# Selective attention and a GELU layer: v before w_in, absmax inside the first layer, batch 1's preparation moved forward

## The chip, the cores and the metric

The kernel runs on one core of one Trainium2 chip. The core has TensorE (PE: matmuls, and weight loads that overlap them), VectorE (DVE), ScalarE (ACT), GpSimd (POOL) and SyncE (SP), each with its own in-order queue of instructions; 16 DMA engines move data, and here GpSimd and SyncE issue nearly all transfers. The metric is the device time of one execution in microseconds; the median of several runs counts. The profile comes from one further execution, taken by the hardware profiler.

## The reference

There are 8 batches of 8 heads, 576 tokens and a head size of 64. The attention's bias falls with the sum of a gate s between two tokens. Its output, 4608 rows of 512, goes through two matrices with a GELU between them.

```python
scores = scale * q @ k.T                       # per head, scale = 1/8
cum = cumsum(maximum(s, 0))                    # along the tokens
scores = where(causal, -1e9, scores + minimum(-(cum[i] - cum[j]), 0))
attn = softmax(scores) @ v                     # exp, sum + 1e-9, divide
x = attn as [B*S, H*D]                         # [4608, 512]
g = 0.5*h*(1 + erf(h/sqrt(2))),  h = x @ w_in  # w_in [512, 2048]
out = g @ w_out                                # w_out [2048, 512]
```

All inputs are fp32, and so is the output.

## The kernel before

The bias splits into a factor of the row, which the softmax's division takes out, and a factor exp(cum[j]) of the column. The kernel makes that factor once for all heads (`cum_sum`, `weights`: a scan on VectorE, transposes on PE with the identity `ident`, exps on ScalarE into `wb`), multiplies v with it (`scale_v`, one VectorE instruction for each of five 128-token tiles, the last of 64 tokens), and keeps the factor itself as a 65th column (`den_col`), so that one matmul gives numerator and denominator. A check of the inputs' sizes guards the split. It needs the largest absolute value of q and k (`absmax`, two VectorE instructions a batch) and the sum of v squared (`square_v`, five ScalarE instructions a batch); a general path, not taken here, stands behind it.

A batch's attention is cut into four score units (g, u): g is one of two groups of four heads, u the first two or the last three token tiles. A unit is: `sc` (matmuls into two PSUM tiles of the tag "sc", of which there are two, and two exps on ScalarE into P), `mk` (the causal mask on VectorE), and `av` items, one for each g and token tile `it` (matmuls of P with the scaled v into a PSUM tile of the tag "av", also two, then a reciprocal and a multiplication on VectorE into x). When both groups of a tile are done, `to_xT` turns x, by PE and a copy or by a DMA transpose on SyncE's queue. q and k are turned by VectorE (`tr_qk`, four transposes a batch) from `raw_qk`, of which there are two buffers; `raw_v` also has two. A buffer's next load waits for all that read it.

The dense part goes in nine chunks of 512 tokens. In chunk c the first layer has eight items `l1_item` (two of 16 column blocks each, 8 matmuls and a GELU on ScalarE); in chunk 0 each item is cut into halves of 256 tokens, because x arrives in pieces. The second layer runs sixteen matmuls for each of four row blocks; `groups` cuts it into pieces and puts the side work of the next batch, b = c + 1, between them from lists `side[i]`. In chunk 0 row blocks 0 and 1 go together in eight groups of four matmuls; group i needs the w_out piece i // 2. Batch 0's attention is written out ahead of chunk 0, with `filler` matmuls on zeros (128x512) in PE's waits.

The order on each engine is that of the text (a manual schedule). GpSimd issues the loads of q, k, v, w_in and w_out; each cast to bf16 but v. It waits for the eighth load before, because eight semaphores go round. Until batch 0's k is cast, the first half of batch 0's k (`k_st`, loaded by SyncE as fp32) lies in batch 0's raw_v buffer, so the v loads over it wait for `cast_k0`. Two GpSimd selects make `ident` and the mask's triangle `uptri`. ScalarE loads an activation table at each change between exp and GELU (`exp_set`, `gelu_set`).

Of the kernel before, what the change touches and what calls it, by code (L numbers as in the profile page):

```python
# [19 lines left out]
def kernel(  # L20
# [10 lines left out]
    nc = tc.nc  # L31
# [10 lines left out]
    ST = 5  # L42
# [62 lines left out]
    def load_qk(b, i, g):  # L105
        t = raw_qk(b)
        for h in range(4):
            nc.gpsimd.dma_start(
                out=t[h * 32 : h * 32 + 32, i, g, :].rearrange("p (t c) -> p t c", c=2 * D),
                in_=qk_runs(q if i == 0 else k, b * H + 2 * h + g, 1),  # L110
            )
# [10 lines left out]
    def raw_v(b):  # L122
        raws[b, "v"] = work.tile([128, ST, H, D], fp32, tag="rawv", bufs=2, name="raw_v")
        return raws[b, "v"]
# [12 lines left out]
            )  # L137


    k_st = raw_v(0).rearrange("p s h d -> p (s h d)")[:, : S * 2]  # L140

    def load_k0():
        for h in range(4):
# [25 lines left out]

    zero = const.tile([128, NB], bf16, name="zero")  # L170
    nc.vector.memset(zero, 0.0)  # L171
    ident = const.tile([128, 128], fp32, name="ident")
    nc.vector.memset(ident, 0.0)
    make_identity(nc, ident, nomemset=True)
# [3 lines left out]
        out=uptri, in_=uptri, compare_op=ALU.is_gt, fill=1.0, base=0, pattern=[[-1, 128]],  # L178
        channel_multiplier=1,
    )  # L180
    load_qk(0, 1, 1)
    amx = const.tile([128, B * HG, 2], fp32, name="amx")
    wb = const.tile([128, ST, BH], bf16, name="wb")
    xT = const.tile([128, NP, n_tok], bf16, name="xT")
# [18 lines left out]
    def masks():  # L203
        nc.vector.tensor_copy(ident_bf, ident)
        nc.vector.tensor_copy(tri_bf, uptri)
# [33 lines left out]
    def den_col(b):  # L239
        nc.vector.tensor_copy(vv[b % 2][:, :, :, D], wb[:, :, b * H : (b + 1) * H])  # L240
# [181 lines left out]
    def filler(n, lhsT=None):  # L422

        f_ps = yps.tile([128, NB], fp32, tag="mlp", bufs=2, name="f_ps")
        for _ in range(n):
            nc.tensor.matmul(  # L426
                f_ps, lhsT=zero[:, :128] if lhsT is None else lhsT, rhs=zero, start=True, stop=True
            )

    def av_item(b, g, it, later=False):  # L430
        P = P_of[b, g]
        n = 128 if it < ST - 1 else SL
        o_ps = ps.tile([128, 4, D + 1], fp32, tag="av", bufs=2, name="av")
        for h in range(4):
            for i, (jt, off) in enumerate(BLK[it]):
                nc.tensor.matmul(  # L436
                    o_ps[:, h, :],
                    lhsT=P[:, h, off : off + 128],
                    rhs=vv[b % 2][:, jt, 2 * h + g, :],
                    start=(i == 0), stop=(i == len(BLK[it]) - 1),  # L440
                )
        if g == 0:
            x_of[b, it] = work.tile([128, H * D], bf16, tag="x", bufs=6, name="x")
        rc = work.tile([128, 4], fp32, tag="rc", bufs=3, name="rc")
        nc.vector.reciprocal(rc[:n], o_ps[:n, :, D])  # L445
        nc.vector.tensor_tensor(  # L446
            x_of[b, it][:n, :].rearrange("p (h g d) -> p g h d", g=HG, d=D)[:, g],
            o_ps[:n, :, 0:D],
            rc[:n].unsqueeze(2).to_broadcast([n, 4, D]),
            op=MULT,  # L450
        )
        if g == HG - 1 and b > 0 and not later:
            to_xT(b, it)
# [57 lines left out]


    exp_set()
    filler(18)
    cum_sum()
    weights()
    den_col(0)
    filler(10)
    cast_k0()

    filler(5, raws[0, "qk"][:, 1, 0, :128])
    load_v(0, nc.gpsimd, (0, 1))
    load_w(0, 0)
    load_w(0, 1)
    load_v(0, nc.gpsimd, (2, 3))
    load_w(0, 2)
    load_w(0, 3)
    load_v(0, nc.gpsimd, (4,))
    load_qks(1)
    load_w(1, 0)  # L530
    load_w(1, 1)
# [6 lines left out]
    tr_qk(0, 0, 1)  # L538
    tr_qk(0, 1, 1)
    masks()  # L540
    filler(2)
    sc_first(1, 0, (0,))
    scale_v(0, 0)
# [6 lines left out]
    sc_first(0, 1, (0,))  # L550
    av_item(0, 0, 1)
    filler(1)
    av_item(0, 1, 0)
    sc_first(0, 1, (1,))
    av_item(0, 1, 1)
    filler(1)
    to_xT(0, 0, True)
    sc_first(1, 1, (0,))
    to_xT(0, 1, True)
    filler(1)  # L560
    sc_first(1, 1, (1,))
    mk_item(0, 0, 1)
    scale_v(0, 2)
# [10 lines left out]
    for c in range(NCH):  # L574
        b = c + 1
        if c > 0 and b + 1 < B:
            load_qks(b + 1)
            load_v(b + 1, nc.gpsimd)
        if c == 0:

            late = [
                [], [(av, 0, 0, 2)], [], [(av, 0, 1, 2)], [(av, 0, 0, 3)],
                [(av, 0, 1, 3), (to_xT, 0, 2, True)], [(to_xT, 0, 3, True)],
                [], [(scale_v, 0, 4)], [], [(av, 0, 0, 4)], [(av, 0, 1, 4), (to_xT, 0, 4)],
            ] + [[]] * 4
            for half in range(2):
                for f2 in range(FT // 2):
                    l1_item(0, f2, half * 256, half * 256 + 256)
                    for f, *a in late[8 * half + f2]:
                        f(*a)  # L590
                    if f2 % 2 and 3 <= 8 * half + f2 <= 9:
                        square_v(0, 4 * half + f2 // 2 - 1)
            for g in range(HG):
                absmax(0, g)
        else:
            for f2 in range(FT // 2):
                l1_item(c, f2)
                for g, it in late_of.get(c, [])[f2 : f2 + 1]:
                    av(c, g, it)
                if b < B and f2 < HG:  # L600
                    tr_qk(b, 0, f2)
                    tr_qk(b, 1, f2)
                if b < B and f2 == 2:
                    den_col(b)
                    for st in range(2):
                        scale_v(b, st)
                if b < B and f2 == 3:
                    for st in range(2, ST):
                        scale_v(b, st)
                if b < B and 4 <= f2 < 4 + HG:  # L610
                    absmax(b, f2 - 4)
                if c == 2 and f2 == 7:
                    cert_decay()
                if c == 1 and 1 <= f2 <= ST:
                    square_v(c, f2 - 1)
        if b < B:
            if c == 0:
                for g in range(HG):
                    for i in range(2):
                        tr_qk(b, i, g)  # L620
                den_col(b)
            exp_set()
            if c == 0:
                side = [[] for _ in range(16)]
                side[0] = [(sc, b, 0, 0), (mk, b, 0, 0)]
                side[2] = [(sc, b, 1, 0), (mk, b, 1, 0)]
                side[3] = [
                    (sc, b, 0, 1), (scale_v, b, 0),
                    (av, b, 0, 0), (scale_v, b, 1), (av, b, 0, 1), (sc, b, 1, 1), (av, b, 1, 0),
                    (scale_v, b, 2), (av, b, 1, 1), (mk, b, 0, 1), (scale_v, b, 3),  # L630
                ]
                side[5] = [(av, b, 0, 2), (mk, b, 1, 1)]
                side[6] = [(av, b, 0, 3)]
                side[8] = [(av, b, 1, 2), (gelu_set,), (square_v, 0, 4)]
                side[9] = [(av, b, 1, 3), (scale_v, b, 4)]
                groups(c, (0, 1), side[:8])
                for sub in (2, 3):
                    groups(c, (sub,), side[4 * sub : 4 * sub + 4])
                load_qks(2)
                load_v(2, nc.gpsimd)  # L640
                for g in range(HG):
                    absmax(b, g)
            else:

                side = [[] for _ in range(16)]
                sc_at = (2, 5, 7, 9) if b < 4 else (2, 5, 8, 11)
                for at, (g, u) in zip(sc_at, [(0, 0), (1, 0), (0, 1), (1, 1)]):
                    side[at].append((sc, b, g, u))
                for st in range(ST):
                    side[sc_at[3]].append((square_v, b, st))  # L650
                side[sc_at[3]].append((gelu_set,))
                for at, (g, u) in zip((5, 8, 10 if b < 4 else 11, 12 if b < 4 else 14), [(0, 0), (1, 0), (0, 1), (1, 1)]):
                    side[at].append((mk, b, g, u))
                for at, (g, it) in zip((6, 7, 9, 10), [(0, 0), (0, 1), (1, 0), (1, 1)]):
                    side[at].append((av, b, g, it))
                if b < 4:
                    side[12].append((av, b, 0, 2))
                    side[13].append((av, b, 1, 2, True))
                    side[14].append((to_xT, b, 2, True))
                if c == 1:  # L660
                    side[3].append((cert_exp,))
                for sub in range(4):
                    groups(c, (sub,), side[4 * sub : 4 * sub + 4])
        else:
            for sub in range(4):
                l2_item(c, (sub,), store=(c, sub) < LAST)
                if c == B - 1:
                    (cert_1, cert_2, cert_3, cert_4)[sub]()
# [172 lines left out]
```

## Time and profile before

| what | value |
|---|---|
| median of 5 runs | 325.93 us (325.04 to 327.14) |
| the profiled execution's own time | 326.16 us |
| its span, first to last instruction | 324.3 us |
| PE busy | 310.4 us, 96% |
| VectorE, ScalarE, GpSimd busy | 191.9, 185.5, 84.0 us |
| mean granted PE clock | 0.989 of full speed |
| loads from HBM, stores to it | 36.85 MB, 9.44 MB |

A row of the timeline has the start, the duration, the engine, the line of the kernel, the operation, out<-in by tile names, the shapes and the number of merged instructions; what stands in brackets is the engine's idle time before it and what ended it. A row by stretch has busy time of each engine, the clock granted to PE, the DMA engines' mean number of packets in flight as a share, and what they moved. A row of waits has who waited, for whom, the sum, the number of waits and the longest.

### The profile page before, as it was taken

The numbers are of one execution on the slowest core, as the hardware profiler recorded it, in microseconds if no ns is written. First come the engines' busy times: TensorE is split into PE (matmuls) and PEld (weight loads), VectorE is DVE, ScalarE is ACT, GpSimd is POOL, SyncE is SP. The second block draws the span as 40 slices with busy tenths as digits, with TensorE's granted clock in tenths as the row PEclk, the third lists the DMA queues.
The fourth block names the chain that finished last, engine by engine and source line by source line (L and its number), as shares of the span: only waits on it lengthen the run. The fifth ranks groups of instructions, "written<-read, shape, count | busy, mean of one in ns | idle before, by whom it ended". The sixth has DMA issues, their size and how long they took to land. (4 is left out here: it accounts for less than half of the span.)

```text
span 324.3 us, 6201 instructions
## 1 busy us (share of the span) xinstructions
PE 310.4 (96%) x2513; PEld 157.0 (48%) x2513; DVE 191.9 (59%) x397; ACT 185.5 (57%) x248; POOL 84.0 (26%) x118
## 2 busy tenths in 40 slices
PE   8899877999999999999999999999999999999994
PEld 3368634444455445544555455545454545444441
DVE  6675747879277957693669466946694632150011
ACT  2577744348785568556585658565856595205500
POOL 8754641461905060506050605000000000000000
PEclk9999977999999999999999999999999999999999
DMA  9999999999997199617945794612111212110012
GB/s 147 160 231 195 219 199 174 166 236 88 193 190 226 20 88 155 204 34 74 170 142 104 82 172 139 107 40 66 66 34 40 60 71 35 40 65 35 1 66 73
DMA packets 67012, 37.36 MB, mean 115 GB/s; under 512 B 54624, under 2 KB 60128, under 8 KB 66976
## 3 DMA queue, kind: packets, MB, share of 16 engines
q0 software_dynamic: 43904, 22.78, 49.5%
q1 hardware_dynamic: 22928, 13.98, 17.1%
q8 instruction: 21, 0.34, 0.4%
q14 instruction: 15, 0.12, 0.1%
q10 hardware_dynamic: 144, 0.13, 0.1%
HBM read 36.85 MB, written 9.44 MB: 143 GB/s over the span
## 5 line engine op out<-in xcount | busy, mean ns | idle before, releaser
L484 PE MATMUL o_ps<-w_out_r,gT 128*128 128x512 bf16 x576 | 137.2, 383 | 0.7 <-ACT o_sb L492 0.5
L468 PE MATMUL h_ps<-xT,w_in_r 128*128 128x512 bf16 (+1 forms) x640 | 132.6, 358 | 0.7 <-DMA xT<-x 0.4
L473 ACT ACTIVATE gT<-h_ps 128x1024 bf16<-128x1024 f32 (+1 forms) x80 | 74.5, 938 | 65.4 <-PE h_ps L468 64.9
L468 PEld LDWEIGHTS <-w_in_r 128*128 128x128 bf16 x640 | 59.8, 98 | 54.9 <-DMA xT<-x 0.9
L484 PEld LDWEIGHTS <-gT 128*128 128x128 bf16 x576 | 52.5, 99 | 60.3 <-issue 6.6
L367 ACT ACTIVATE P<-sc_ps 128x1024 bf16<-128x1024 f32 x56 | 54.3, 1021 | 35.2 <-PE sc_ps L352 35.2
L494 DVE COPY o_sb<-o_ps 128x512 f32<-128x512 f32 x32 | 22.1, 691 | 58.6 <-PE o_ps L484 58.6
L130 POOL DMA_DIRECT2D raw_v<-in_v_dram x40 | 34.1, 869 | 61.5 <-ACT sq L224 59.4
L445 DVE RECIPROCAL rc<-av 128x4 f32<-128x4 f32 (+1 forms) x80 | 14.3, 179 | 43.8 <-PE av L436 43.5
L216 DVE TENSOR_REDUCE amx<-raw_qk 128x2 f32<-128x2304 bf16 x16 | 40.2, 2535 | 0.0
L436 PEld LDWEIGHTS <-P 128*128 128x128 bf16 x576 | 28.0, 98 | 18.4 <-issue 2.1
L446 DVE TENSOR_TENSOR x<-av,rc 128x256 bf16<-128x256 f32 (+1 forms) x80 | 33.8, 423 | 3.0 <-DVE rc L445 0.3
L117 POOL DMA_DIRECT2D raw_qk<-in_q_dram x32 | 21.8, 685 | 49.4 <-DVE amx L216 38.4
L436 PE MATMUL av<-vv,P 128*128 128x65 bf16 x576 | 31.0, 195 | 2.6 <-DVE vv L232 2.0
L375 DVE TENSOR_TENSOR P<-P,tri_bf 128x1024 bf16<-128x1024 bf16 x32 | 22.0, 686 | 10.3 <-ACT P L367 10.3
L232 DVE TENSOR_TENSOR vv<-raw_v,wb 128x512 bf16<-128x512 f32 (+1 forms) x40 | 26.0, 690 | 2.4 <-DMA raw_v<-in_v_dram 2.4
L224 ACT ACTIVATE sq<-raw_v 128x512 bf16<-128x512 f32 (+1 forms) x40 | 24.6, 624 | 0.0
L209 DVE STREAM_TRANSPOSE qkT<-raw_qk 128x576 f32<-128x576 f32 x32 | 22.6, 749 | 0.4 <-DMA raw_qk<-in_q_dram 0.4
L352 PE MATMUL sc_ps<-qkT 32*128 32x256 bf16 (+2 forms) x560 | 19.1, 258 | 3.0 <-DVE qkT L209 2.2
L117 POOL DMA_DIRECT2D raw_qk<-in_k_dram x28 | 18.9, 676 | 5.9 <-DMA w_in_r<-in_moe_w_in_dram 3.5
L352 PEld LDWEIGHTS <-qkT 32*128 32x128 bf16 x560 | 12.3, 94 | 15.5 <-issue 11.4
L426 PE MATMUL f_ps<-zero 128*128 128x512 bf16 x42 | 12.7, 419 | 1.2 <-DVE zero L171 1.2
(78 smaller groups left out, 93.0 us busy)
## 6 DMA issues: line engine op xcount, KB each, us to landing
out_dram<-o_sb SPq DMA_DIRECT2D x35, 256.0 KB, 2.5
raw_v<-in_v_dram POOLq DMA_DIRECT2D x32, 256.0 KB, 4.7
raw_qk<-in_q_dram POOLq DMA_DIRECT2D x32, 144.0 KB, 6.0
raw_qk<-in_k_dram POOLq DMA_DIRECT2D x28, 144.0 KB, 6.6
w_in_r<-in_moe_w_in_dram POOLq DMA_DIRECT2D x4, 512.0 KB, 10.2
w_out_r<-in_moe_w_out_dram POOLq DMA_DIRECT2D x4, 512.0 KB, 12.5
raw_v<-in_v_dram POOLq DMA_DIRECT2D x8, 128.0 KB, 5.4
raw_v<-in_k_dram SPq DMA_DIRECT2D x4, 144.0 KB, 4.6
```

The source lines that it names most:

```text
L117: nc.gpsimd.dma_start(out=t[h * 32 : h * 32 + 32, i, :, :].rearrange("p g (t c) -> p (g t) c", c=2 * D), in_=qk_runs(q if i == 0 else k, b ...
L130: eng.dma_start(out=t[:n_st, st, :, :], in_=bass.AP(tensor=v.tensor, offset=v.offset + b * H * S * D + st * 128 * D, ap=[[D, n_st], [S * D ...
L216: nc.vector.tensor_reduce(amx[:, b * HG + g], raws[b, "qk"][:, :, g, :], axis=AX, op=ALU.max, apply_absolute_value=True,)
L224: nc.scalar.activation(sq[:n_st], raws[b, "v"][:n_st, st].rearrange("p h d -> p (h d)"), func=AF.Square, accum_out=sumv[:n_st, b, st : st ...
L232: nc.vector.tensor_tensor(vv[b % 2][:n_st, st, :, 0:D], raws[b, "v"][:n_st, st, :, :], w.unsqueeze(2).to_broadcast([n_st, H, D]), op=MULT,)
L352: nc.tensor.matmul(s_ps[h // 2][:, h % 2, off : off + n], lhsT=qk[r, 1, g, jt * 128 : jt * 128 + 128, e], rhs=qk[r, 0, g, i0 : i0 + n, e], ...
L367: nc.scalar.activation(P[:, 2 * h2 : 2 * h2 + 2, o : o + 512], s_ps[h2], func=AF.Exp, scale=scale)
L436: nc.tensor.matmul(o_ps[:, h, :], lhsT=P[:, h, off : off + 128], rhs=vv[b % 2][:, jt, 2 * h + g, :], start=(i == 0), stop=(i == len(BLK[it ...
L446: nc.vector.tensor_tensor(x_of[b, it][:n, :].rearrange("p (h g d) -> p g h d", g=HG, d=D)[:, g], o_ps[:n, :, 0:D], rc[:n].unsqueeze(2).to_ ...
L468: nc.tensor.matmul(h_ps[:, i, :], lhsT=w_in_r[:, ko, ft * 128 : (ft + 1) * 128], rhs=xT[:, ko, c * NB + n0 : c * NB + n1], start=(ko == 0) ...
L473: nc.scalar.activation(gT_of[c][:, f2 * 2 : f2 * 2 + 2, n0:n1], h_ps, func=AF.Gelu)
L484: nc.tensor.matmul(y_of[c, sub], lhsT=gT[:, ft, sub * 128 : (sub + 1) * 128], rhs=w_out_r[:, ft, :], start=(ft == 0), stop=(ft == FT - 1),)
```

## The change

1. The odd heads' k of batch 0 and the first v tile are issued on GpSimd ahead of the two selects; `k_st` moves to the end of the raw_v buffer, over tiles 2 to 4. The other v tiles go ahead of all of w_in.
2. `den_col(0)` moves behind the masks; fillers move (18, 10 and 5 become 28 and 4; one of 1 becomes 2); one score half goes ahead of an av item.
3. In chunk 0's first layer the av items of tiles 2 to 4 move forward, both `absmax` of batch 0 go into the ninth half item, and the last `square_v` of batch 0 comes in from the second layer.
4. In chunk 0's second layer `scale_v` of batch 1's tiles 0 and 1 goes to the first two score units, the last score unit behind the first tiles' av items, and `idle` matmuls on zeros (128x256, into "av" tiles) go between them.

```diff
-    k_st = raw_v(0).rearrange("p s h d -> p (s h d)")[:, : S * 2]
+    k_st = raw_v(0).rearrange("p s h d -> p (s h d)")[:, ST * H * D - S * 2 :]
...
     nc.vector.memset(zero, 0.0)
+    load_qk(0, 1, 1)
+    load_v(0, nc.gpsimd, (0,))
     ident = const.tile([128, 128], fp32, name="ident")
...
-    load_qk(0, 1, 1)
...
+    def idle(n):
+
+        f_ps = ps.tile([128, 256], fp32, tag="av", bufs=2, name="i_ps")
+        for _ in range(n):
+            nc.tensor.matmul(f_ps, lhsT=zero[:, :128], rhs=zero[:, :256], start=True, stop=True)
...
-    filler(18)
+    filler(28)
     cum_sum()
     weights()
-    den_col(0)
-    filler(10)
     cast_k0()
 
-    filler(5, raws[0, "qk"][:, 1, 0, :128])
-    load_v(0, nc.gpsimd, (0, 1))
-    load_w(0, 0)
-    load_w(0, 1)
-    load_v(0, nc.gpsimd, (2, 3))
-    load_w(0, 2)
-    load_w(0, 3)
-    load_v(0, nc.gpsimd, (4,))
+    filler(4, raws[0, "qk"][:, 1, 0, :128])
+    load_v(0, nc.gpsimd, (1, 2, 3, 4))
+    for i in range(4):
+        load_w(0, i)
...
     masks()
+    den_col(0)
...
+    sc_first(0, 1, (1,))
     av_item(0, 1, 0)
-    sc_first(0, 1, (1,))
...
-    filler(1)
+    filler(2)
     sc_first(1, 1, (1,))
...
-                [], [(av, 0, 0, 2)], [], [(av, 0, 1, 2)], [(av, 0, 0, 3)],
-                [(av, 0, 1, 3), (to_xT, 0, 2, True)], [(to_xT, 0, 3, True)],
-                [], [(scale_v, 0, 4)], [], [(av, 0, 0, 4)], [(av, 0, 1, 4), (to_xT, 0, 4)],
-            ] + [[]] * 4
+                [], [(av, 0, 0, 2)], [(av, 0, 1, 2)], [(av, 0, 0, 3)],
+                [(av, 0, 1, 3), (to_xT, 0, 2, True)], [(scale_v, 0, 4)], [(to_xT, 0, 3, True)],
+                [(av, 0, 0, 4)], [(av, 0, 1, 4), (to_xT, 0, 4), (absmax, 0, 0), (absmax, 0, 1)],
+            ] + [[]] * 7
...
-                    if f2 % 2 and 3 <= 8 * half + f2 <= 9:
+                    if f2 % 2 and 3 <= 8 * half + f2 <= 11:
                         square_v(0, 4 * half + f2 // 2 - 1)
-            for g in range(HG):
-                absmax(0, g)
...
-                side[0] = [(sc, b, 0, 0), (mk, b, 0, 0)]
-                side[2] = [(sc, b, 1, 0), (mk, b, 1, 0)]
+                side[0] = [(sc, b, 0, 0), (mk, b, 0, 0), (scale_v, b, 0)]
+                side[2] = [(sc, b, 1, 0), (mk, b, 1, 0), (scale_v, b, 1)]
                 side[3] = [
-                    (sc, b, 0, 1), (scale_v, b, 0),
-                    (av, b, 0, 0), (scale_v, b, 1), (av, b, 0, 1), (sc, b, 1, 1), (av, b, 1, 0),
-                    (scale_v, b, 2), (av, b, 1, 1), (mk, b, 0, 1), (scale_v, b, 3),
+                    (sc, b, 0, 1), (idle, 6), (av, b, 0, 0), (av, b, 0, 1), (scale_v, b, 2), (idle, 4),
+                    (av, b, 1, 0), (av, b, 1, 1), (mk, b, 0, 1), (sc, b, 1, 1), (scale_v, b, 3), (idle, 4),
                 ]
...
-                side[8] = [(av, b, 1, 2), (gelu_set,), (square_v, 0, 4)]
+                side[8] = [(av, b, 1, 2), (gelu_set,)]
```

## The prediction

> **What bounds the kernel now.** I read the busy shares first, then the waits of TensorE, then time cut at the program's own stages.
>
> ```profile
> PE 310.4 (96%) x2513; PEld 157.0 (48%) x2513; DVE 191.9 (59%) x397; ACT 185.5 (57%) x248; POOL 84.0 (26%) x118
> ...
> PEclk9999977999999999999999999999999999999999
> DMA  9999999999997199617945794612111212110012
> ```
>
> TensorE is the bound on average, and the only dips of its clock and nearly all of the dense DMA lie in the first quarter. Stage by stage (columns: stretch in us, its length, busy time and count on PE, weight loads, VectorE, ScalarE, GpSimd, granted clock, DMA share, GB/s):
>
> ```profile
> 11.40:21.65 10.25, 9.63 (x126) 5.59 (x127) 7.55 (x19) 7.07 (x8) 7.27 (x10) 1.00 1.06 211
> 21.65:28.80 7.15, 6.88 (x85) 5.98 (x83) 4.46 (x14) 6.15 (x11) 2.64 (x4) 1.00 1.39 210
> 28.80:38.67 9.87, 9.62 (x100) 8.46 (x100) 5.90 (x10) 7.19 (x17) 7.82 (x10) 1.00 1.49 184
> 38.67:56.08 17.41, 12.43 (x136) 6.27 (x137) 11.59 (x22) 9.43 (x10) 6.02 (x9) 0.80 1.47 205
> 56.08:66.64 10.56, 9.69 (x70) 4.54 (x67) 8.77 (x15) 3.52 (x6) 4.22 (x5) 1.00 1.06 183
> 66.64:319.60 252.96, 252.81 (x1965) 122.49 (x1965) 146.06 (x303) 149.27 (x196) 47.49 (x65) 1.00 0.52 97
> ```
>
> From 66.64 on PE idles 0.15 us in 253, so what the first 66.64 us gain reaches the end whole, unless a new wait appears. The loose stage is 38.67 to 56.08: second layer of chunk 0 with batch 1's score units between its groups. PE idles 5 us there, and its clock is halved for two spells. The waits of PE from 21 us on name the causes:
>
> ```profile
> PE sc_ps L352 <- DVE qkT L209: 2.2, 1, 2.2
> PE av L436 <- DVE vv L232: 2.0, 2, 1.3
> PE sc_ps L352 <- ACT P L367: 0.6, 1, 0.6
> ```
>
> and the timeline (start, duration, engine, line) shows the first of them:
>
> ```profile
> 35.52 4.99 DVE L216 TENSOR_REDUCE amx<-raw_qk 128x2 f32<-128x2304 bf16 x2
> ...
> 40.44 2.74 DVE L209 STREAM_TRANSPOSE qkT<-raw_qk 128x576 f32<-128x576 f32 x4
> ...
> 41.92 1.04 PE L352 MATMUL sc_ps<-qkT 32*128 32x256 bf16 x16 [2.21 <-DVE qkT L209]
> ```
>
> Two absmax instructions (2.5 us each) stand ahead of batch 1's transposes on the in-order VectorE, and PE waits for the second transpose.
>
> **Part 1, the load order.** The trace's landing times tell what the GpSimd queue delivers, in order: k of odd heads 11.52, v0 13.45, v1 15.82, w_in 0 and 1 at 19.45 and 22.02, v2 22.76, v3 23.55, w_in 2 and 3 at 25.96 and 28.76, v4 29.18, batch 1's q and k 35.50, w_out 0 and 1 at 38.63 and 43.08, v of batch 1 44.23 to 47.07, w_out 2 and 3 at 49.44 and 51.95. From 12 to 55 us this stream has no pause, but between 11 and 12 us it nearly runs dry, since v0 waits for the cast of k to leave its buffer and is issued at 10.02. Now k's staging lies over v2 to v4, and the queue issues: q until 4.10 as before, k of odd heads (4 x 0.62) to 6.58, v0 (0.90) to 7.5. v0 then streams right behind k and lands near 12.5, so the stream gains about 0.9 us. v1 goes out at 9.2, v2 waits for the cast (10.1), v3, v4 follow, then w_in from 12.7 on. Everything up to v4 is the same bytes, so w_in 3, now last of them, lands at 29.18 - 0.9 = 28.3 instead of 28.76. w_in 0 has v2 to v4 ahead of it (0.74 + 0.79 + 0.42 by the landing steps) and lands near 20.5, before PE wants it at 21.5.
>
> The two GpSimd selects are pushed behind these issues: ident is ready at 7.85, not 4.52, uptri at 9.2, not 5.84. The weights' transposes on PE start after 28 fillers at about 8.4 (6.50 before), their exps end at 9.4, the cast of k on ACT runs 9.4 to 10.1 (9.05 to 9.73 before). The cover is q's landing at 9.84: VectorE transposes q until 10.7 and only then needs k. Cost nothing; without that cover 0.4 us. Fillers are 32 for 33 in the opening, in the same waits; the one more at the end of the attention part costs 0.2. den_col (0.33) moves behind the masks: VectorE has 0.5 idle there. The early attention stays bound by PE and ACT in turn; I give it nothing either way (-0.3 to +0.5).
>
> **Part 2, the first layer of chunk 0.** PE reaches its seventh item at 28.81 just as w_in 3 has landed. With 28.3 that is 0.45 earlier; behind it stand the same ten half items, so the layer ends at 38.0 instead of 38.45, and w_out 0 (37.7) is there. The av items move a slot earlier without the wait for v2 (0.8 of VectorE, no PE). Two squares (0.62 + 0.19 each) lie in ScalarE's spare time, about 0.3 us per item, and are made up by the layer's end. The two absmax now follow av(1, 4) on VectorE: PE does that at about 32.1, so they run 33.0 to 38.0, and nothing that PE or ACT need before 38 is queued behind them. Batch 1's k has landed (35.50 - 0.9). The four transposes take 38.0 to 40.75, the first score unit can start after two of them, at 39.4.
>
> **Part 3, groups and score units.** Group 0 runs 38.1 to 39.1, the score unit 39.4 to 40.1, group 1 to 41.0. Then what was late behind the transposes appears: group 2 wants w_out 1, at 43.08 - 0.9 = 42.2. It ends 43.1, and unit (1, 0) starts there instead of at 45.67: **2.55 us**. From there I counted on: its exps to 45.7 (1.94), mask 0.7 and v scaling 1 (0.69) to 47.15, unit (0, 1) 45.75 to 46.4, six idle matmuls (0.11 each) to 47.05, av 0 and 1 until 47.75, their divisions (0.18 + 0.42 each) to 48.65. idle takes the "av" PSUM buffers in turn, so av of group 1 waits for that division: 48.7 to 49.35; unit (1, 1) 49.4 to 50.1, four idles, group 4 at 50.6, av 2 behind the mask (51.55) at 52.45, group 6 at 52.9. That is 9.8 us from unit (1, 0) to group 6, and 56.08 - 45.67 = 10.4 before: **0.6**. scale_v 0 and 1 are now off this path, but the idle matmuls' buffers take back much of it.
>
> The clock belongs here. Rows by clock window:
>
> ```profile
> 38.02:41.44 3.42, 1.44 (x8) 0.42 (x6) 3.42 (x4) 2.04 (x3) 0.75 (x1) 1.00 1.37 258
> 41.44:44.85 3.41, 2.93 (x21) 1.18 (x22) 1.95 (x4) 1.86 (x2) 1.01 (x2) 0.50 0.91 201
> 48.26:51.68 3.42, 1.34 (x38) 1.17 (x41) 2.51 (x5) 1.96 (x3) 0.68 (x2) 1.00 1.61 187
> 51.68:55.09 3.41, 3.41 (x41) 2.06 (x38) 2.68 (x8) 1.94 (x2) 0.66 (x1) 0.50 1.81 179
> ```
>
> A window in which PE is busy 1.44 or 1.34 of 3.4 us is followed by one at half clock. The Trainium skill ("TensorE: Matmul & The Clock Gate", "Why this matters for your kernels") asks only for no idle gap above some 3 us. By it the longest gap, 2.2, is harmless and the 14 idle matmuls buy nothing; the two half windows would have another cause, stay, and take 2 us off the sum below (325.0). By the row each half window costs about 1 us: groups 4 and 5, eight matmuls, took 2.84, where 24 later took 5.34 (1.8 for eight). I go by the row. My count keeps every window over half busy, so full clock is in the 9.8 us; one half window left over would cost 1.
>
> **Part 4, after group 6.** 10.56 us of dense groups stay. square_v(0, 4) leaves ScalarE's queue there (0.82, not on the path), and frees batch 0's v buffer 27 us earlier: the v loads of batch 2 (issued 60.96, after 8.07 of GpSimd's wait) go directly behind q and k of batch 2. The last two DMA transposes of x (61.94 to 66.60 for the last; PE waits 0.4 for it) will be issued near 58.7, PE wants them at 63.1. They now meet the tail of q and k rather than v; the two of 53.62 and 54.85, which met q and k, took 6.8 and 5.9 us. At 5.9 the wait is 1.5 instead of 0.4, at 4.7 as before; nearer is 4.7, since q and k are mostly through, and I take 0.25. to_xT of tile 4 moves from 35.62 to about 32.4 on the otherwise empty SP queue; its data moved from 39 to 45.6, when w_out 1 took 4.45 us instead of 3.1. That delay falls on batch 1's k or w_out 0 now: at worst w_out 0 comes at 39.6 and unit (1, 0) 0.1 to 0.7 later. Sum: 2.55 + 0.6 - 0.25 = **2.9 us** (part 1 and 2 are inside the 2.55). The profiled execution took 326.16 around a span of 324.3; it would become 323.3. The five runs' median is 325.93, so I predict **323.0**.
>
> **Rivals.** *The stream is the bound*: w_out 1 to 3 keep their landing times, because the moved DMA transpose holds the rings longer and the 0.9 is not gained. For it: landings at 43.08 and 51.95 against needs of 41.0 and 52. Then unit (1, 0) starts at 44.0 to 44.7: 1.2 us gained, 324.7. *No delay by the transpose*: w_out 1 at 40.6; unit (1, 0) is then held by ACT (42.1), the gain is 4.9, 321.0. Against it: every DMA transpose that met a casting load here was slow. *The edits cancel*: PE waits for x what it gained: 325.9; that takes a landing 3 us later than I count.
>
> *Slower*: the v tiles before w_in are dear. v1 landed 2.37 us after v0, v2 and v3 at steps of 0.74 and 0.79. If each of v1 to v4 costs 2.37, they take 8.3 for 4.3 before; the skill ("DMA: Bandwidth & Descriptors", "Anatomy of one DMA") would give bytes / 436 GB/s = 0.6 for each, and w_in 0 0.45 us earlier than I have it. I take the steps of 0.75, since v1 came out of an empty queue. At 2.37 w_in 3 and w_out 1 come 3.1 late instead of 0.9 early, unit (1, 0) at 47.1, and PE waits in the first layer, with a half window: 327. It turns slower when a v tile costs more than about 2.1.
>
> **Numbers.** Main case 0.48 (own range 321.8 to 324.0), stream 0.20, no delay 0.12, cancelled 0.07, slower 0.13. Timing here tells 0.3% (1 us) from nothing: below 324.95 lie the main case, no delay and 0.14 of the stream, 0.74; the rest of the stream and cancelled, 0.13, are within; slower 0.13. The range 320.7 to 326.3 leaves out most of the slower case and the tail of the low one.
>
> **What would show it.** Right: absmax ends before 39, PE's wait for qkT below 0.5, a wait of about 1 us for w_out ahead of group 2, no half clock after 4 us, first layer of chunk 1 at 63.7. Wrong: w_in 3 after 29.5; a PE wait for x above 2 us; a wait for vv still there; idle matmuls waiting for av's division by more than 1 us.

## The result, and the profile after

The changed kernel's median is 325.66 us beside 326.23 us for the kernel before, measured together; the ratio is 0.9969 (95% interval 0.9953 to 0.9985), a gain of about 1.0 us. This ratio, like those below, leaves out slow executions (more than 1.5% above the fastest of their own kernel: 10 of 42 of the changed kernel, 2 of 79 of the kernel before), while with all of them the medians differ by 0.6 us and the means (326.1 and 326.2) hardly at all. The prediction was 2.9 us (ratio 0.991): the direction was right, a third of the size came at best. In a second comparison the ratio was 0.996 (0.9938 to 0.9981).

The profiled execution took 324.06 us with a span of 322.3, so it is 2.0 us of span ahead of the one shown of before. Two things stand between the trace and the 2.9 us, a wait that the trace shows and the clock in other executions, and both start at the same place. First the page of after, its rows of busy shares, clock and DMA:

```profile
PE 309.2 (96%) x2527; PEld 157.2 (49%) x2527; DVE 191.9 (60%) x397; ACT 185.2 (57%) x248; POOL 82.7 (26%) x118
...
PEclk9999999999999999999999999999999999999999
DMA  9999999992998097709954995412101221010012
```

The two dips of the clock are gone. The stages of after, cut at its own borders (start of the second layer of chunk 0, its group 6, start of chunk 1's first layer; only 28.80 is kept from before; columns as in the rows before):

```profile
28.80:38.50 9.70, 9.46 (x101) 8.55 (x101) 6.97 (x9) 7.70 (x18) 7.90 (x10) 1.00 1.49 183
38.50:51.52 13.02, 11.50 (x152) 6.56 (x150) 9.26 (x21) 9.63 (x10) 5.32 (x9) 1.00 1.33 230
51.52:64.19 12.67, 9.69 (x70) 4.55 (x66) 9.32 (x14) 3.07 (x4) 5.42 (x7) 1.00 1.39 248
64.19:317.50 253.31, 252.83 (x1965) 122.41 (x1965) 145.47 (x302) 149.14 (x195) 46.24 (x64) 1.00 0.51 94
```

The stage up to group 6 shrank from 17.41 to 13.02 us: group 6 starts at 51.52 instead of 56.08, a gain of 4.56 us. The next stage grew from 10.56 to 12.67, and 2.1 us of the gain are given back. The waits of PE from 21 us on say to whom:

```profile
PE h_ps L475 <- DMA xT<-x: 2.5, 1, 2.5
PE sc_ps L353 <- ACT P L368: 1.0, 2, 0.6
PE h_ps L475 <- ACT gT L480: 0.7, 1, 0.7
```

The waits for qkT (2.2) and vv (2.0) are gone, and PE's wait for x ahead of chunk 1 rose from 0.4 to 2.5. The rows of SyncE's and GpSimd's queues and the matmul that waits, first of before:

```profile
58.66 0.85 SPq L496 DMA_DIRECT2D out_dram<-o_sb  x2
60.66 2.51 SPq L413 DMA_TRANSPOSE xT<-x  x2
60.96 4.27 POOL L130 DMA_DIRECT2D raw_v<-in_v_dram  x5 [8.07 <-ACT sq L224]
66.64 1.90 PE L468 MATMUL h_ps<-xT,w_in_r 128*128 128x512 bf16 x8 [0.40 <-DMA xT<-x]
```

and of after:

```profile
49.08 2.50 SPq L414 DMA_TRANSPOSE xT<-x  x2
51.50 0.90 POOL L130 DMA_DIRECT2D raw_v<-in_v_dram  x1 [0.46 <-ACT P L368]
52.55 2.64 POOL L130 DMA_DIRECT2D raw_v<-in_v_dram  x3 [0.15 <-issue]
54.10 0.86 SPq L503 DMA_DIRECT2D out_dram<-o_sb  x2
55.46 0.70 POOL L130 DMA_DIRECT2D raw_v<-in_v_dram  x1 [0.27 <-DMA raw_qk<-in_q_dram]
56.10 3.01 SPq L414 DMA_TRANSPOSE xT<-x  x2
...
64.19 1.90 PE L475 MATMUL h_ps<-xT,w_in_r 128*128 128x512 bf16 x8 [2.52 <-DMA xT<-x]
```

Batch 2's v is now issued from 51.50 on (60.96 before), three of its five tiles ahead of the stores and all of them ahead of the last two transposes of x. These v loads land 7.7 to 8.3 us after their issue, the last at 63.44, so they are in flight while the stores and the transposes are. By the trace's landing times the two stores issued at 54.10 and 54.58 land at 61.21 and 63.48 (before: 2.7 and 2.8 us after their issue), the transposes of 56.10 and 57.38 at 63.70 and 64.15, 7.6 and 6.8 us after their issue (before: 4.0 and 4.7).

The second thing is the clock. A half window here is a stretch of 3.41 us at half clock. The recorded mean clock of each execution tells about how many it had: one takes 0.005 off (half of 3.41 in 322 us), and half clock behind the last matmul took up to 0.004 in these traces. Of the 66 executions of the changed kernel in both comparisons, 36 lie at 0.996 or above and have a median of 324.5 us, 25 with about one half window (0.990 to 0.995) have 326.4, and 5 lie lower, with 330.3. The trace shown is one of the first kind. Of 93 executions of the kernel before, none is at 0.996 or above; 50 with about one half window have 325.3, 43 with about two 326.8.

### The profile page after: what moved, and what is told of

Read it like the earlier page. It is cut to its first block, busy times and chain, and to the rows that moved or that the text cites. A ratio compares the mean times of both kernels' runs of the same rounds, so it can differ in the third digit from the quotient of the medians.

```text
span 322.3 us, 6228 instructions
## 1 busy us (share of the span) xinstructions
PE 309.2 (96%) x2527; PEld 157.2 (49%) x2527; DVE 191.9 (60%) x397; ACT 185.2 (57%) x248; POOL 82.7 (26%) x118
## 5 line engine op out<-in xcount | busy, mean ns | idle before, releaser
L491 PE MATMUL o_ps<-w_out_r,gT 128*128 128x512 bf16 x576 | 135.3, 379 | 0.5 <-ACT o_sb L499 0.5
L443 PE MATMUL av<-vv,P 128*128 128x65 bf16 x576 | 30.3, 194 | 0.1
## 6 DMA issues: line engine op xcount, KB each, us to landing
w_out_r<-in_moe_w_out_dram POOLq DMA_DIRECT2D x4, 512.0 KB, 10.8
```

The source lines that it names most:

```text
L443: nc.tensor.matmul(o_ps[:, h, :], lhsT=P[:, h, off : off + 128], rhs=vv[b % 2][:, jt, 2 * h + g, :], start=(i == 0), stop=(i == len(BLK[it ...
L491: nc.tensor.matmul(y_of[c, sub], lhsT=gT[:, ft, sub * 128 : (sub + 1) * 128], rhs=w_out_r[:, ft, :], start=(ft == 0), stop=(ft == FT - 1),)
```

## The experiments

**The changed kernel once more**, as a control for the next three.

> The changed kernel once more, to stand beside the others on one chip. Its trace had PE waiting 2.5 us for the DMA transposes of x ahead of chunk 1's first layer, and no half clock; its median was 1 us below before. Half-clock theory: the wait for x is long enough to leave a clock window mostly idle in part of the executions, so that a trace of another execution can show one half window (3.4 us at half clock, 1.7 us lost) right behind the wait, and the time is 324.3 without and 326 with it. Rival: the wait for x itself varies by some us and no half window follows it.

Median 324.84, ratio 0.996. Its trace repeats the first: group 6 at 51.42, wait for x 2.63, no half window. A later variant with the same wait (the changed kernel with reordered loads, below; that execution took 326.81 us) does show the window:

```profile
62.52:65.93 3.41, 0.86 (x5) 0.21 (x3) 1.72 (x1) 0.60 (x1) 1.40 (x3) 1.00 1.26 245
65.93:69.35 3.42, 3.42 (x14) 1.37 (x13) 0.00 (x0) 0.07 (x1) 3.42 (x6) 0.50 1.41 170
```

A window with 0.86 us of PE work, the wait for x, is followed by one at half clock in the dense part, where nothing hides it. That the 30 executions of the changed kernel below 0.996 had theirs at this place is a conclusion from their clock, from this trace and from the counts of the variants below; none of them left a trace of its own.

**Batch 2's v later.** `square_v(0, 4)` is the last reader of the buffer that batch 2's v goes into. In the first variant it goes back behind group 8 (the edit of side[8] below), in the second behind group 11 (that of side[11]):

```diff
-                    if f2 % 2 and 3 <= 8 * half + f2 <= 11:
+                    if f2 % 2 and 3 <= 8 * half + f2 <= 9:
...
-                side[8] = [(av, b, 1, 2), (gelu_set,)]
+                side[8] = [(av, b, 1, 2), (gelu_set,), (square_v, 0, 4)]
...
                 side[9] = [(av, b, 1, 3), (scale_v, b, 4)]
+                side[11] = [(square_v, 0, 4)]
```

> The changed kernel with square_v(0, 4) back behind group 8 of the second layer, which holds batch 2's v loads back to about 56 us (51.5 in the changed kernel, 61.0 before). Theory v-early: the v loads that come out early hold up the stores and the x transposes queued behind them on SyncE; with them back the stores land by 57 and the last transpose about 62.5 to 63, PE waits 0.4 to 1.2 instead of 2.5, and the time falls 1.5 to 3 us against the changed kernel. Rival q-and-k: the transposes are slow because they meet the casting loads of batch 2's q and k, which stay where they are; the wait stays at 2 or more and the time stays. Rival own-latency: PE has simply become earlier than a transpose can be; the wait stays at 2 or more.

> As the last one, but square_v(0, 4) stands behind group 11, so that batch 2's v is issued near 59, after both x transposes. Theory v-early: the transposes have the rings to themselves and land near 60 to 61; PE's wait for x is below 0.3 and the time falls 2.5 to 4 us against the changed kernel, if v (landing near 65) is still early enough for its scaling. Rivals q-and-k and own-latency: PE's wait stays at 2 or more, the time stays.

The first: median 323.56, ratio 0.9923 (0.9895 to 0.9951). The v loads go out at 57.24, the transposes land 5.5 and 5.6 us after issue, PE waits 1.3, and 3 of 14 executions lie below 0.996. The second: 321.95, ratio 0.9873 (0.9835 to 0.991), 2.9 us below the changed kernel by medians. Its timeline has the order of before again:

```profile
55.09 0.85 SPq L503 DMA_DIRECT2D out_dram<-o_sb  x2
57.09 2.50 SPq L414 DMA_TRANSPOSE xT<-x  x2
...
60.75 4.28 POOL L130 DMA_DIRECT2D raw_v<-in_v_dram  x5 [9.10 <-ACT sq L225]
62.51 1.89 PE L475 MATMUL h_ps<-xT,w_in_r 128*128 128x512 bf16 x8
```

The matmul of chunk 1 has no wait, and none of its six executions has a half window. The early v is the cause of the lost part. (The edit also takes one square out of the first layer; the next experiment leaves it there and gains too.) It is not all of the delay: with v out of the way the stores of 55.09 still take 5.3 and 5.5 us (2.7 and 2.8 before), when q and k of batch 2 and two earlier transposes are in flight. The rival's part is there, but it is not on the path.

**Two tiles turned by PE.** The v loads stay early:

```diff
-                side[8] = [(av, b, 1, 2), (gelu_set,)]
-                side[9] = [(av, b, 1, 3), (scale_v, b, 4)]
+                side[8] = [(av, b, 1, 2, True), (gelu_set,)]
+                side[9] = [(av, b, 1, 3, True), (to_xT, b, 2, True), (scale_v, b, 4)]
+                side[11] = [(to_xT, b, 3, True)]
```

> The changed kernel with tiles 2 and 3 of batch 1's x turned by PE and copied by VectorE (eight more transposes, 0.2 us of PE and 0.42 of VectorE for each tile) in place of the two DMA transposes; v loads stay early. All theories that see the lost time in the wait for x: the wait falls below 0.3, PE starts chunk 1's first layer near 62.2, and the time falls 2 to 4 us against the changed kernel (322 to 323.5). If the lost time lies elsewhere (first layer of chunk 0, batch 2's own preparation), the time falls less than 1 us.

Median 322.50, ratio 0.9912 (0.9889 to 0.9936): 2.3 us below the changed kernel by medians, 1.6 by the ratios. Chunk 1 starts at 62.86 without a wait. (This trace lost 1.7 us elsewhere, waiting for w_out ahead of the second layer.) The half windows go with the wait: 1 of 19 executions lies below 0.996, beside 30 of 66 of the changed kernel, though v comes as early in both. So the wait for x, however it is removed, is what the change lost.

**absmax back behind the first layer.** From here on the base is the second v variant.

```diff
-                [(av, 0, 0, 4)], [(av, 0, 1, 4), (to_xT, 0, 4), (absmax, 0, 0), (absmax, 0, 1)],
+                [(av, 0, 0, 4)], [(av, 0, 1, 4), (to_xT, 0, 4)],
...
+            for g in range(HG):
+                absmax(0, g)
```

> From here on the base is the kernel with square_v behind group 11, whose PE does not wait for x, so that what an edit is worth reaches the end. This one puts both absmax of batch 0 back behind the first layer. By the prediction's sum: they run 38.5 to 43.5 on the base's time scale, the transposes after them, PE's wait for qkT of about 2.2 us is back, unit (1, 0) is some 2 us later, time 1.5 to 2.5 us above the base, or more with a half clock window behind that wait. Rival (the w_out stream is the bound there): the wait for qkT replaces waits for w_out and ScalarE, and the time rises by less than 0.7.

A miss: 321.91, ratio 0.9856 (0.9817 to 0.9895), the same as the base (321.95, 0.9873). VectorE's timeline shows why:

```profile
34.15 4.99 DVE L217 TENSOR_REDUCE amx<-raw_qk 128x2 f32<-128x2304 bf16 x2
39.06 2.74 DVE L210 STREAM_TRANSPOSE qkT<-raw_qk 128x576 f32<-128x576 f32 x4
...
40.89 0.63 PE L353 MATMUL sc_ps<-qkT 32*128 32x256 bf16 x16
```

Between av(1, 4) and the transposes VectorE has nothing else, so absmax runs right behind the av item wherever the text puts it (34.12 on the base, 34.15 here). What moved it from 35.52 to 33.14 was mainly the av item's move from the twelfth half item to the ninth. In the variant with the old lists and early loads (below) v4 has landed at 27.2 and absmax still starts at 34.84; with the new lists and that order of loads from v1 on (the reordered base below) it starts at 32.46.

**No idle matmuls.**

```diff
-                    (sc, b, 0, 1), (idle, 6), (av, b, 0, 0), (av, b, 0, 1), (scale_v, b, 2), (idle, 4),
-                    (av, b, 1, 0), (av, b, 1, 1), (mk, b, 0, 1), (sc, b, 1, 1), (scale_v, b, 3), (idle, 4),
+                    (sc, b, 0, 1), (av, b, 0, 0), (av, b, 0, 1), (scale_v, b, 2),
+                    (av, b, 1, 0), (av, b, 1, 1), (mk, b, 0, 1), (sc, b, 1, 1), (scale_v, b, 3),
```

> The base without the 14 idle matmuls between batch 1's score units. Clock theory: PE is busy less than 1.9 of 3.4 us in a window there, in part of the executions a half window comes back, and the time rises 0.3 to 1 us, with more executions below full clock. Rival (the Trainium skill's rule of gaps of 3 us and more): no half window, and since the idle matmuls hold the av buffers (0.4 us of wait each round) the time falls 0 to 0.5.

Median 321.99, ratio 0.9846 (0.9791 to 0.99): inconclusive alone; of its six executions four are at full clock and two are not (0.995 and 0.973). The last experiment repeats it on the better load order.

**The side lists of before** on the base:

```diff
-                side[0] = [(sc, b, 0, 0), (mk, b, 0, 0), (scale_v, b, 0)]
-                side[2] = [(sc, b, 1, 0), (mk, b, 1, 0), (scale_v, b, 1)]
+                side[0] = [(sc, b, 0, 0), (mk, b, 0, 0)]
+                side[2] = [(sc, b, 1, 0), (mk, b, 1, 0)]
                 side[3] = [
-                    (sc, b, 0, 1), (idle, 6), (av, b, 0, 0), (av, b, 0, 1), (scale_v, b, 2), (idle, 4),
-                    (av, b, 1, 0), (av, b, 1, 1), (mk, b, 0, 1), (sc, b, 1, 1), (scale_v, b, 3), (idle, 4),
+                    (sc, b, 0, 1), (scale_v, b, 0),
+                    (av, b, 0, 0), (scale_v, b, 1), (av, b, 0, 1), (sc, b, 1, 1), (av, b, 1, 0),
+                    (scale_v, b, 2), (av, b, 1, 1), (mk, b, 0, 1), (scale_v, b, 3),
                 ]
```

> The base (square_v behind group 11) with batch 1's side lists of before: scale_v 0 and 1 between the av items, the last score unit ahead of them, no idle matmuls. By the prediction's sum this part is worth 0.6 us. Now that neither absmax's place nor the idle matmuls has shown a worth alone, this is what is left to have removed PE's two waits for vv (2.0 us) and the second half window: if so the waits are back, a half window in most executions, and the time rises 1.5 to 2.5. If it is the w_out stream that sets group 4 and 6, it rises less than 0.6.

The waits and the half window are back as the theory had it; the size is less sure. The median is 323.61, 1.7 us above the base, but by the ratio, 0.9899 (0.9862 to 0.9936), it is 0.8 us, and the intervals overlap. PE waits 2.0 for vv, and five of six executions have a half window. From the start of unit (1, 0) to group 6 the trace takes 10.8 us for 9.3 on the base. All of these 1.5 us are the clock, in the eight matmuls of groups 4 and 5, here and on the base:

```profile
50.42 3.45 PE L491 MATMUL o_ps<-w_out_r,gT 128*128 128x512 bf16 x8
50.54 1.89 PE L491 MATMUL o_ps<-w_out_r,gT 128*128 128x512 bf16 x8
```

So without the half window the new lists would have gained nothing on this stretch: the waits for vv that they remove are made up by idle matmuls and other waits.

**The order of the loads.** On the base the loads from v1 on go in the order of before; in a second variant the same is done on the changed kernel itself:

```diff
-    load_v(0, nc.gpsimd, (1, 2, 3, 4))
-    for i in range(4):
-        load_w(0, i)
+    load_v(0, nc.gpsimd, (1,))
+    load_w(0, 0)
+    load_w(0, 1)
+    load_v(0, nc.gpsimd, (2, 3))
+    load_w(0, 2)
+    load_w(0, 3)
+    load_v(0, nc.gpsimd, (4,))
```

> The base with the loads in the order of before from v1 on (v1, w_in 0 and 1, v2, v3, w_in 2 and 3, v4), all else as changed. If v ahead of w_in is worth something by itself: VectorE's scaling of tile 4 now waits for v4 near 29 us, the turns of x behind it come late, the first layer ends later, time up 0.5 to 1.5. If only the number of bytes ahead of w_in 3 counts: w_in 3 lands 0.2 to 0.7 earlier, the layer ends within 0.3 of the base's, time within 0.5.

> The changed kernel (square_v early, so batch 2's v early) with only the order of loads of before from v1 on. Cause under test: v2 to v4 ahead of w_in hold all of w_in behind the cast of k on GpSimd's in-order queue, and the stream runs dry from 11 to 13 us. Expected: w_in 3 near 25.4 instead of 29.0, w_out 3 near 47, no wait for w_in or w_out; PE still waits for x behind the early v loads (2 us or more), so the time is 0.5 to 1.5 us below the changed kernel, not at 321. If the stream's earlier end also clears the rings for the transposes, the wait for x falls below 1 and the time goes to 321 to 322.

The first gives 320.71, ratio 0.9827 (0.979 to 0.9865), the best but for the last. Its interval overlaps the base's (0.9835 to 0.991), but its six executions (320.1 to 321.6) all lie below five of the base's six (321.7 to 323.0). The expectation asked about the bytes ahead of w_in 3 and missed the point: w_in 3 lands at 25.4, not 0.2 to 0.7 earlier than 29 to 30, and w_out 0 at 34.7 instead of 39.8. GpSimd's queue in the changed kernel:

```profile
7.93 0.96 POOL L130 DMA_DIRECT2D raw_v<-in_v_dram  x1
10.94 2.46 POOL L130 DMA_DIRECT2D raw_v<-in_v_dram  x3 [2.06 <-ACT raw_qk L150]
13.39 3.00 POOL L168 DMA_DIRECT2D w_in_r<-in_moe_w_in_dram  x4
```

and in the variant:

```profile
7.91 0.95 POOL L130 DMA_DIRECT2D raw_v<-in_v_dram  x1
9.47 1.54 POOL L168 DMA_DIRECT2D w_in_r<-in_moe_w_in_dram  x2 [0.61 <-DMA raw_qk<-in_q_dram]
11.11 1.78 POOL L130 DMA_DIRECT2D raw_v<-in_v_dram  x2
```

v2 lies over k's staging and waits 2 us for ScalarE's cast. All of w_in is queued behind it in the changed kernel, and two of its pieces go ahead of it in the variant and fill the stream in the meantime. From 12 to 13 us the DMA engines moved 82 GB/s in the changed kernel and 212 in the variant. By landing times v2 to v4 came at steps of 1.5, 1.5 and 0.7 us in the changed kernel and 0.7, 0.8 and 0.4 in the variant, and w_in 0 followed the v tile ahead of it by 4.0 us for 2.4: together 3.3 of the 3.6 us. On the changed kernel the order gives 324.46, ratio 0.9908 (0.9875 to 0.9941), 0.5 to 0.6% below it. It keeps the wait for x (2.55 in its trace) and the half windows (6 of 13 executions below 0.996), so the two losses are separate. The second half of its expectation, a stream so early that the transposes are free, did not come.

**The cast ahead of the weights' transposes.** On the base, ScalarE's cast that frees k's staging goes ahead of the transposes of the gate's weights, so that v2 can go out earlier, and tile 4 of x is turned by PE, one half item later:

```diff
-                [(av, 0, 0, 4)], [(av, 0, 1, 4), (to_xT, 0, 4), (absmax, 0, 0), (absmax, 0, 1)],
-            ] + [[]] * 7
+                [(av, 0, 0, 4)], [(av, 0, 1, 4)], [(to_xT, 0, 4, True), (absmax, 0, 0), (absmax, 0, 1)],
+            ] + [[]] * 6
...
-    weights()
     cast_k0()
+    weights()
```

> The base with two edits for a better version: batch 0's tile 4 of x is turned by PE (its DMA transpose meets the loads of w_out; PE's wait for w_out ahead of the second layer was 0.2 to 1.7 us in the traces so far), and the cast of k stands ahead of the weights' exps on ScalarE (v2 to v4 waited for it until 10.9 us with the stream near dry). Expected: v2 lands near 13.5 and w_in 3 0.5 to 0.9 earlier, PE's wait for w_out below 0.3, time 0.5 to 1.5 us below the base. If the w_out stream is set by the bytes ahead of it alone: within 0.3 of the base.

Median 321.22, ratio 0.9838 (0.9801 to 0.9876), beside 321.95 and 0.9873 for the base: the medians differ by 0.7 us, the intervals overlap, so it is unclear. The steps did move: v2 landed at 14.4 (14.8 on the base, 13.5 expected), w_in 3 at 28.87 (29.98 on the base) and w_out 0 at 37.88 (39.78), PE waits 0.2 us for w_in in place of 0.8, and no longer for w_out. The reordered queue moves the same loads further (w_in 3 at 25.4).

**The loads alone.** On the kernel before, only k of the odd heads and v0 go ahead of the selects and k's staging to the buffer's end; the order of v and w_in stays.

```diff
-    k_st = raw_v(0).rearrange("p s h d -> p (s h d)")[:, : S * 2]
+    k_st = raw_v(0).rearrange("p s h d -> p (s h d)")[:, ST * H * D - S * 2 :]
...
+    load_qk(0, 1, 1)
+    load_v(0, nc.gpsimd, (0,))
     ident = const.tile([128, 128], fp32, name="ident")
...
-    load_qk(0, 1, 1)
...
-    load_v(0, nc.gpsimd, (0, 1))
+    load_v(0, nc.gpsimd, (1,))
```

> The kernel before with only the first half of the load change: k of the odd heads and v0 ahead of the selects and k's staging at the buffer's end; the order of v and w_in stays. Expected: w_in 3 near 25.5 instead of 28.8, w_out 1 near 38 instead of 43; but av of tile 4 stays in the twelfth item, absmax and the transposes behind it, so PE waits about 2.5 us for qkT and 2 for vv and two half windows stay: 0.3 to 1.2 us below before. If the loads were the bound of the stage from 38.7 to 56: 2 us or more below.

Median 325.85, ratio 0.9983 (0.9963 to 1.0003): w_in 3 lands at 26.7, w_out 1 at 39.2, and hardly anything comes of it, since PE still waits 2.6 for qkT, 2.0 for vv and 1.5 for x. So the loads were not what bound the stage while the waits on VectorE stood.

**The best order without idle matmuls**: the edit of the no-idle variant on the reordered base.

> The best kernel so far (square_v behind group 11, loads in the order of before from v1 on) without the 14 idle matmuls. If they buy nothing: within 0.5 us of 320.7, PE's waits for the av buffers (0.4) gone and small waits for vv in their place, no half window. If the clock needs them once w_out no longer holds PE: 0.5 to 1 us slower, some executions below full clock.

Median 320.35, ratio 0.9799 (0.9759 to 0.9838), level with 0.9827. But the six executions fall into two sorts: three at full clock (319.2, 319.5, 319.6) and three with a half window (321.2, 321.7, 322.3). The trace is of the second sort:

```profile
44.75:48.16 3.41, 1.90 (x45) 1.32 (x45) 2.53 (x7) 2.70 (x3) 0.66 (x1) 1.00 1.78 180
48.16:51.57 3.41, 3.41 (x38) 1.72 (x36) 2.83 (x8) 1.95 (x3) 0.00 (x0) 0.50 1.84 184
```

With the idle matmuls none of six had one, a difference that six executions each do not settle alone. By the medians they cost about 1.2 us when the clock would have held (320.7 for 319.5) and save about 1.0 when it would not (321.7), so in the middle they are worth nothing here.

Both reordered versions beat both kernels: 320.7 and 320.4 beside 325.7 and 326.2.

## Why the prediction was wrong in size

**Part 4 is the step that failed.** The prediction saw that batch 2's v would go out right behind q and k, and still wrote of the last two transposes: "They now meet the tail of q and k rather than v". It took 4.7 us from issue to landing and 0.25 us more of PE's wait for x, with 5.9 and a wait of 1.5 as the other end. In the trace they met all five v tiles, which land from 59.20 to 63.44; the transposes took 7.6 and 6.8 us, PE waited 2.5, and the term was 2.1. The sum also left out what stands ahead of the transposes on their own queue: two stores, which now share the DMA engines with 1.2 MB of v and land 7 to 9 us after their issue. How much of the delay came by way of the stores and how much from v directly is open: with v at 57.24 the stores landed at 60.4 and 61.1, as they did with v later still, and the transposes took 5.5 for 4.6 and 3.8. The wait has a follow-up that no term of the sum had: it empties a clock window, and 30 of 66 executions have a half window, 25 of them with a median 1.8 us higher (326.4 for 324.5). The prediction counted half windows only between groups 0 and 6. It had a wait for x above 2 us among its signs of being wrong, and listed "PE waits for x what it gained" at 0.07.

**Part 1 failed in its gain, and the reason was in view.** ident was ready at 7.8 (7.85 predicted), v0 landed at 12.2 (12.5), w_in 0 at 20.6 (20.5). But w_in 3 landed at 29.0, not 28.3. The fillers ran at half clock (0.43 us each) until 4.64, 0.7 us longer than in the trace of before, the weights' transposes came at 9.03 and not 8.4, and the cast behind them on ScalarE's queue at 9.97, so v2 went out at 10.94 and not 10.1. "Cost nothing" was said of the cast's delay for VectorE's side; the GpSimd queue behind the cast was named and priced at the time of v2 alone. "Everything up to v4 is the same bytes" hid that an order can leave the stream dry: with two pieces of w_in ahead of v2 the same bytes were through 3.2 us earlier (25.81 for 29.00), and w_in 3 by 3.6. So the first layer gained nothing (38.5 for 38.1 predicted and 38.67 before).

**Part 2 was right in its times and not in what it named.** absmax ran 33.14 to 38.13 (33.0 to 38.0), the transposes from 38.05, the first unit at 39.53 (39.4). The place of absmax in the text did none of this; the av items did.

**Part 3 was low.** Unit (1, 0) began at 41.93 and went on at 42.60, held by ScalarE and not by w_out 1, which landed at 40.75 and not at 42.2. That is the rival "no delay by the transpose" (w_out 1 at 40.6, the unit held by ScalarE at 42.1), given 0.12; the rival of a stream that is the bound did not come true. From there to group 6 it took 9.6 us (9.8 predicted, 10.4 before), and of the 0.8 gained 0.95 is the clock: groups 4 and 5 took 1.89 us for 2.84. Group 6 came at 51.52 instead of 52.9. On the base the side lists are worth 0.8 us by the ratios and 1.7 by the medians for the 0.6 given, again by the clock and not by the waits for vv. The half windows of this stage went away as the rows of before suggested.

**The slower rival** (v tiles at 2.37 each) was wrong: v2 to v4 landed at steps of 1.5, 1.5 and 0.7 even with the late issue of v2, and w_in 3 came 0.2 us late and not 3.1.

In sum, by the traces: 4.56 us gained up to group 6 for 3.15 predicted, 2.1 given back for 0.25, and 0.4 more behind the last matmul, where the kernel took 5.3 us to its end for 4.8 before (4.4 to 5.5 in the traces here); that leaves 2.0 in this pair of executions. The windows of the clock fall differently in each execution, and the ratio leaves 1.0 us.

## What to carry to other kernels

When an edit frees a buffer earlier, follow the load that was waiting for it: list what it will now run beside, and on each other queue the transfers that stand ahead of the one that the critical engine waits for. On an in-order queue do not put a load that must wait for a conversion ahead of loads that could go; equal bytes are not equal time if the order lets the stream run dry. And moving an instruction in the text moves it on the chip only if something stands between its old and its new place on its engine.

## What the runs showed of the hardware

The clock can be halved after a window of 3.4 us in which PE works too little in sum, with no long gap needed. In the last trace the longest single gap of PE in the window was 0.63 us, its busy time was 1.90 of 3.41, and the next window ran at half clock; the variant with the old side lists had 1.84, and so had its next window halved. But the busy time alone does not decide. Other windows with as little were not followed by a half window: 1.89 in the trace of after (62.67 to 66.08), 1.85 in the trace with early loads (36.76 to 40.17), and 1.71 with two tiles turned by PE:

```profile
38.01:41.42 3.41, 1.71 (x23) 0.66 (x22) 2.50 (x5) 1.88 (x2) 0.75 (x1) 1.00 1.14 247
41.42:44.83 3.41, 3.41 (x32) 1.42 (x28) 1.30 (x2) 2.71 (x3) 2.00 (x4) 1.00 1.10 281
```

The windows that were followed by one had 0.86, 1.34, 1.41, 1.44, 1.84 and 1.90; those of 1.34, 1.41, 1.84 and 1.90 hold mostly short score and av matmuls, the three that were not followed by one mostly long ones. Whether the kind of matmul counts is not tested here, so no limit can be given. The Trainium skill ("TensorE: Matmul & The Clock Gate", "Why this matters for your kernels") asks for no idle gaps above some 3 us; here windows with gaps of 0.2 to 0.6 us were enough, and the measurement decides.

A store of 256 KB on SyncE's queue landed 2.7 and 2.8 us after its issue in the kernel before, where the loads of q and k were ending, 5.3 and 5.5 beside these loads in the second variant with v later, and 7.1 and 8.9 with v in flight too in the changed kernel. A DMA transpose of one x tile took 4.0 and 4.7, 4.6 and 3.8, and 7.6 and 6.8 us in the same three kernels; in the kernel before it ran beside the v loads, with the stores landed early (61.3 and 62.0).
